# First block's feed-forward in plain float32, and the split of its weights moved eight units later

## The chip, the cores and the metric

One core of a Trainium2 chip runs the whole program. The metric is the device time of one execution in microseconds (us). Three runs of the kernel before took 1052.34, 1054.83 and 1055.13 us, median 1054.83. Readings come from one more execution with the hardware profiler on: 1054.6 us, of which the profile spans 1052.9.

## The reference

Three stages follow each other. A delta rule over 768 steps for 4 x 8 heads of width 48, then two feed-forward networks on 3072 tokens (model width 384, hidden width 2048):

```python
for t in range(S):
    y[:, :, t] = einsum('bhd,bhde->bhe', q[:, :, t], state)
    v_old = einsum('bhde,bhd->bhe', state, k_n[:, :, t])
    state = state + beta_t * einsum('bhd,bhe->bhde', k_n[:, :, t], v_t - v_old)
# x: the y of all heads, (3072, 384)
h = x @ w_in;  g = h if h >= 1, 0 if h <= -1, else (h + 1)**2 / 4;  x2 = g @ w_out
h = x2 @ w2_in; r = max(h, 0); out = (r * r) @ w2_out
```

All is float32, except that the weights reach the kernel as int64 bit patterns of float64 values, two 32-bit words for each weight.

## The kernel before

**The delta rule** goes in 24 chunks of 32 steps. A chunk needs the inverse of a 32x32 triangular matrix for every batch and head. `tri` makes these for a group of chunks at once: DVE (the VectorE) normalises the gram matrix, and then some 30 dependent steps multiply and add ever other shapes of it, each step one multiply (L411) and one add (L412). Group 0 (two chunks) is done on DVE in two half-size inverses side by side and put together with two small matmuls (`joined`: z at L437, w at L445). All other groups go through the steps on GpSimd (POOL). With the inverse, `chunk_steps` runs a chunk as six pieces: ks and tr (the new values u), qs and pu (the output y), ku (the state in PSUM, tiles `sps`), xt (y transposed to x). The pieces of a chunk follow each other through PE, ACT and DVE.

**The feed-forward** goes in blocks of 2 or 3 chunks (256 or 384 tokens). A block has 16 units, one for each 128 hidden columns: `hidden` (h, three K tiles of 128) and, two units later (LAG), `out1` (three output tiles in PSUM, `acc`). A float32 product is made of three float32r products: x and w are each split in a rounded part and a remainder (`xh`, `xl`; the two halves of `weight`; `gh`, `gl`), and `prods` issues hi*hi, lo*hi, hi*lo: 9 matmuls for h, 9 for acc. The chunks of the next block run between the units of this one, so the first block (chunks 0 and 1) has to wait for nothing but its own two chunks, and the units of block 0 and 1 also carry the work that follows.

**The weights.** 32 tiles (16 units x 2 matrices) of the first network are loaded as raw words (`load_w`, L157, 384 KB each), turned into float32 by one ACT instruction (L164) and two DVE instructions (L172, L175), and split by one ACT copy (L186) and one DVE subtraction (L190). Eighteen loads are asked for at the start (EAGER), the others as conversions go on (AHEAD). The second network's weights are converted later and wait in DRAM (w2f).

**What sets the order.** Up to the first `manual_schedule` block's end every engine follows the written order. After it PE alone follows the written order, and a scheduler orders the other engines' queues by its own model of their times. Each engine runs its queue in order, so an instruction that waits holds all behind it. SP issues the DMAs, also in order. Work that is hung on unit slots (`put`, two slots for each unit; `later` puts it behind that unit's own instructions) sets when the next chunks, the inverses and the weights come.

Of the kernel before, what the change touches and what calls it, by code (L numbers as in the profile page):

```python
# [25 lines left out]
def kernel(  # L26
# [38 lines left out]
    EAGER = 18  # L65
    AHEAD = 8
# [48 lines left out]
    kqt, kvt, gp, nt, xh, xl = {}, {}, {}, {}, {}, {}  # L115

# [31 lines left out]
    raws = {}  # L148


    def load_w(x, key):
# [5 lines left out]
        nc.sync.dma_start(raw.rearrange("p a b -> p (a b)"), (w1, w2)[w][f, i].bitcast(I32))  # L157


    def convert_stages(key, box):  # L160
        def s0():
# [6 lines left out]
        def s1():  # L168
# [13 lines left out]
    def part_stages(key, box):  # L182
        _, f, i = key

        def s3():
            nc.scalar.copy(weight(i, f)[0], box["t"])  # L186

        def s4():
            hi, lo = weight(i, f)
            nc.vector.tensor_sub(lo, box["t"], hi.bitcast(F32))  # L190

        return convert_stages(key, box) + [s3, s4]
# [3 lines left out]
    def weight_items(w):  # L196
# [5 lines left out]
        def item(x):  # L202
            _, f, i = keys[x]
            box = {}
            if w == 0:
                r = part_stages(keys[x], box)
            else:
                r = convert_stages(keys[x], box)
                r.append(lambda: nc.sync.dma_start(w2f[f, :, i], box["t"]))
            s1 = r[1]  # L210
            r[1] = lambda: (s1(), ahead(x + 1 + (RAW if w else AHEAD)))
# [5 lines left out]
        def ahead(end):  # L217
            while todo and todo[0][0] < end:
# [49 lines left out]
    def gram(c, lo=0, hi=2, late=0, eng=None):  # L268
# [18 lines left out]
        if c >= KQ:  # L287
            kqg.pop(c)
            if late < 2:
# [23 lines left out]
    spare = {  # L313
        name: f"w{i}{NF - f}" for name, i, f in
        (("u0", 1, 1), ("u1", 1, 2), ("cross", 0, 1), ("z", 1, 3), ("l", 0, 2), ("d", 1, 4))
    }
# [17 lines left out]
    def tri(n, eng, halves=False):  # L334
# [9 lines left out]
        def two(t, rows, cols):  # L344

            a = t[:, rows, cols]
            (ps_, p_), (rs_, r_), (cs_, c_) = a.ap
            return bass.AP(a.tensor, a.offset, [[ps_, p_], [T2 * (T + 1), 2], [rs_, r_], [cs_, c_]])

# [5 lines left out]
        both = slice(0, T2)  # L355
# [16 lines left out]

        def row():
            if halves:
                d = two(gm, both, both)
                eng.tensor_mul(
                    d, d, r.rearrange("p (a o i) -> p a o i", a=2, o=1)
                    .to_broadcast([P, 2, T2, T2]))
                return
            for e, rs, cs in whole:  # L380
                e.tensor_mul(gm[:, rs, cs], gm[:, rs, cs], across(r, rs, cs))

        def row2():
            if halves:
                eng.tensor_mul(
                    two(x, both, both), two(gm, both, both),
                    g.rearrange("p (a i o) -> p a i o", a=2, o=1).to_broadcast([P, 2, T2, T2]))
            else:
                for e, rs, cs in whole:
                    e.tensor_mul(x[:, rs, cs], gm[:, rs, cs], down(g, rs, cs))  # L390
# [5 lines left out]
        def step(j):  # L396
            if halves:
                w = T2 - 1 - j
                t = ring.tile([P, 2, j, w], F32, tag="t0", bufs=1, name="t")
                rest = two(x, slice(0, j), slice(j + 1, T2))  # L400
                by = two(x, slice(0, j), slice(j, j + 1))
                of = two(gm, slice(j, j + 1), slice(j + 1, T2))
                shape = [P, 2, j, w]
            else:
                w = T - 1 - j
                t = ring.tile([P, j, w], F32, tag="t0", bufs=1, name="t")
                rest = x[:, 0:j, j + 1:T]
                by = x[:, 0:j, j:j + 1]
                of = gm[:, j:j + 1, j + 1:T]
                shape = [P, j, w]  # L410
            eng.tensor_mul(t, by.to_broadcast(shape), of.to_broadcast(shape))  # L411
            eng.tensor_add(rest, rest, t)  # L412
# [44 lines left out]
    def chunk_steps(c):  # L457
# [75 lines left out]
        def xt():  # L533
            if j == 0:
                xh[n] = ring.tile([P, KT, P * SIZES[n]], F32R, tag="xh", bufs=2, name="xh")
# [6 lines left out]
            nc.scalar.copy(xh[n][:, :, cols], o)  # L542
            marks[2] = nc.vector.tensor_sub(xl[n][:, :, cols], o, xh[n].bitcast(F32)[:, :, cols])  # L543
# [19 lines left out]
    marks = [None, None, None]  # L563

    def hidden(layer, n, f):
# [4 lines left out]
        wi = weight(0, f)  # L570
        cols = [slice(kt * P, (kt + 1) * P) for kt in range(KT)]
        prods([
            (h, (wi[0][:, c], wi[1][:, c]), (xh[n][:, kt], xl[n][:, kt]), kt == 0, kt == KT - 1)
            for kt, c in enumerate(cols)
        ])
        r = ring.tile([P, w], F32, tag="rg", bufs=RG, name="r")
        g = ring.tile([P, w], F32, tag="rg", bufs=RG, name="g")
        if layer == 0:
# [10 lines left out]
        def rest():  # L589
            ghi = ring.tile([P, w], F32R, tag="gh", bufs=GB, name="gh")  # L590
# [12 lines left out]
    def out1(n, f):  # L603
        w = P * SIZES[n]
        if f == 0:
            acc[n] = [ps.tile([P, w], F32, tag=f"acc{m}", name=f"acc{m}") for m in range(KT)]
        g = gs.pop((0, n, f))
        wo = weight(1, f)
        cols = [slice(m * P, (m + 1) * P) for m in range(KT)]
        prods([  # L610
            (acc[n][m], (wo[0][:, c], wo[1][:, c]), g, f == 0, f == NF - 1)
            for m, c in enumerate(cols)
# [294 lines left out]
```

## Time and profile before

| | |
|---|---|
| median of three runs | 1054.83 us |
| profiled execution: time, span | 1054.6 us, 1052.9 us |
| PE busy (matmul) | 989.3 us, 94% |
| DVE busy | 611.5 us, 58% |
| ACT busy | 454.3 us, 43% |
| POOL busy | 313.2 us, 30% |
| first h matmul of block 0 | at 65.68 us |
| first h matmul of block 1 | at 137.93 us |
| first h matmul of block 2 | at 199.90 us |

Times in the profile are microseconds from the start of the span. PE works through two records for one small float32 matmul and one record for one float32r matmul. "issue" behind a row is time in which the engine waited for nothing that the profile shows.

### The profile page before, as it was taken

The page shows a single profiled execution, that of the slowest core. Times are in us where ns is not written, and L with a number is a line of the kernel's source. Part 1 is how long each engine was busy: PE and PEld are TensorE (multiplying, and loading weights), DVE is VectorE, ACT ScalarE, POOL GpSimd, SP SyncE. Part 2 cuts the span into 40 slices and gives each one's busy share as a digit, 9 for nine tenths or more (in the row PEclk, how much of TensorE's full clock was granted, in tenths as well). Part 3 has the DMA queues.
Part 4 walks back from the last instruction along what each step waited for, and adds up shares of the span by engine and source line. Part 5 has one row for each costly group of instructions (what it writes and reads, how often), then busy time and mean ns, then how long its engine had stood idle before and what let it go on. Part 6 is the DMA issues. An engine that isn't in the chain of part 4 may idle for free.

```text
span 1052.9 us, 33012 instructions
## 1 busy us (share of the span) xinstructions
PE 989.3 (94%) x14440; PEld 945.0 (90%) x14440; DVE 611.5 (58%) x1125; ACT 454.3 (43%) x931; POOL 313.2 (30%) x456
## 2 busy tenths in 40 slices
PE   4358898999999999999999999999999999999998
PEld 4347788898899998999999999999999999999998
DVE  6879765675575666767545577543434343444333
ACT  2346544445444444545445554433333333333332
POOL 4690681294039208608600123110101010010000
PEclk9997999999999999999999999999999999999999
DMA  9942144352451441512111223010101010000000
GB/s 297 326 121 77 33 124 134 88 150 73 130 152 48 148 134 33 167 56 70 31 42 55 77 90 121 16 45 1 45 1 46 1 45 1 24 1 24 1 23 23
DMA packets 36049, 80.89 MB, mean 77 GB/s; under 512 B 4544, under 2 KB 18368, under 8 KB 35904
## 3 DMA queue, kind: packets, MB, share of 16 engines
q1 hardware_dynamic: 35904, 78.78, 24.8%
q8 instruction: 113, 1.85, 0.8%
q14 instruction: 32, 0.26, 0.1%
HBM read 63.03 MB, written 15.73 MB: 75 GB/s over the span
## 4 chain that ended last, share of the span: by engine, by line
PE 81%; DVE 11%; issue 4%; ACT 2%; DMA 1%; SPq 0%; DVEq 0%; ACTq 0%
PE acc L555 36%; PE h L555 35%; PE tr L486 2%; PE yy L506 2%; PE sps L517 2%; PE yy L472 2%; DVE g L582 1%; DVE g L584 1%; PE g L281 1%; PE ks L472 1%; DVE gl L593 1%; DVE wl L172 1%; DVE wl L175 1%; DVE gp L415 1%; PE xt L540 1%
## 5 line engine op out<-in xcount | busy, mean ns | idle before, releaser
L555 PE MATMUL h<-xh,w 128*128 128x384 f32 (+1 forms) x1632 | 320.4, 332 | 1.8 <-ACT r L581 1.3
L555 PEld LDWEIGHTS h<-xh,w 128*128 128x128 f32 x1632 | 272.7, 190 | 6.8 <-ACT r L581 1.8
L593 DVE TENSOR_TENSOR gl<-g,gh 128x384 fp32r<-128x384 f32 (+1 forms) x272 | 169.5, 623 | 134.3 <-ACT gh L592 128.8
L592 ACT CAST gh<-g 128x384 fp32r<-128x384 f32 (+1 forms) x272 | 135.0, 496 | 209.3 <-DVE g L584 106.0
L555 PE MATMUL h<-xl,w 128*128 128x384 f32 (+1 forms) x816 | 179.8, 329 | 1.3 <-DVE xl L543 1.3
L555 PE MATMUL acc<-gh,w 128*128 128x384 f32 (+1 forms) x864 | 168.5, 331 | 3.8 <-ACT gh L592 3.8
L587 DVE TENSOR_TENSOR g<-r 128x384 f32<-128x384 f32 x128 | 71.4, 558 | 157.4 <-ACT r L586 157.4
L555 PE MATMUL acc<-w,gh 128*128 128x384 f32 x768 | 155.6, 337 | 2.0 <-DVE e L600 2.0
L586 ACT ACTIVATE r<-h,zero 128x384 f32<-128x384 f32 x128 | 74.5, 582 | 166.1 <-PE h L555 166.1
L555 PEld LDWEIGHTS acc<-gh,w 128*128 128x128 f32 x864 | 136.9, 191 | 9.8 <-ACT gh L592 4.2
L555 PEld LDWEIGHTS h<-xl,w 128*128 128x128 f32 x816 | 141.5, 190 | 1.9 <-DVE xl L543 1.9
L555 PEld LDWEIGHTS acc<-w,gh 128*128 128x128 f32 x768 | 136.3, 188 | 2.3 <-ACT gh L592 2.3
L581 ACT ACTIVATE r<-h,one 128x384 f32<-128x384 f32 (+1 forms) x144 | 78.6, 546 | 89.4 <-PE h L555 84.9
L411 POOL TENSOR_TENSOR t<-tx,gm 128x30 f32<-128x30 f32 (+9 forms) x180 | 109.6, 609 | 19.9 <-DVE tx L390 6.4
L412 POOL TENSOR_TENSOR tx<-tx,t 128x30 f32<-128x30 f32 (+9 forms) x180 | 108.4, 602 | 13.7
L584 DVE SCALAR_TENSOR_TENSOR g<-r,g 128x384 f32<-128x384 f32 (+1 forms) x144 | 88.8, 617 | 36.6 <-ACT g L583 34.8
L582 DVE TENSOR_SCALAR g<-r 128x384 f32<-128x384 f32 (+1 forms) x144 | 63.6, 442 | 79.5 <-ACT r L581 78.9
L642 POOL CAST xh<-x2r 128x1152 fp32r<-128x1152 f32 x8 | 9.5, 1186 | 292.9 <-PE h L555 246.1
L583 ACT ACTIVATE g<-g 128x384 f32<-128x384 f32 (+1 forms) x144 | 70.6, 490 | 59.4 <-DVE g L582 58.3
L555 PE MATMUL acc<-gl,w 128*128 128x384 f32 (+1 forms) x432 | 91.5, 320 | 2.6 <-DVE gl L593 2.6
L555 PE MATMUL acc<-w,gl 128*128 128x384 f32 x384 | 88.0, 337 | 0.0
L555 PEld LDWEIGHTS acc<-gl,w 128*128 128x128 f32 x432 | 72.4, 190 | 3.3 <-DVE gl L593 3.3
(94 smaller groups left out, 835.9 us busy)
## 6 DMA issues: line engine op xcount, KB each, us to landing
raw<-in_w_dram SPq DMA_DIRECT2D x64, 384.0 KB, 6.3
kqt<-in_kq_dram SPq DMA_DIRECT2D x88, 192.0 KB, 3.8
kv<-in_kv_dram SPq DMA_DIRECT2D x24, 384.0 KB, 3.1
w2f<-wl SPq DMA_DIRECT2D x32, 192.0 KB, 3.5
w2r<-w2f SPq DMA_DIRECT2D x16, 384.0 KB, 3.0
x2r<-x SPq DMA_DIRECT2D x8, 576.0 KB, 4.4
out_dram<-e SPq DMA_DIRECT2D x24, 192.0 KB, 2.0
x<-e SPq DMA_DIRECT2D x18, 192.0 KB, 2.3
```

The costliest lines, as they stand in the source:

```text
L411: eng.tensor_mul(t, by.to_broadcast(shape), of.to_broadcast(shape))
L412: eng.tensor_add(rest, rest, t)
L472: per_bh(lambda b, h, p, pd: nc.tensor.matmul(o[p, h], kqt[c][pd, b // 2, h, x * T:(x + 1) * T], st[pd, b // 2, h], start=h == 0, stop=x = ...
L555: nc.tensor.matmul(o, *((r, l) if swap else (l, r)), **flags)
L581: marks[0] = nc.scalar.activation(r, h, AF.Relu, bias=one)
L582: marks[1] = nc.vector.tensor_scalar(g, r, 2.0, 0.5, ALU.min, ALU.mult)
L583: nc.scalar.activation(g, g, AF.Square)
L584: nc.vector.scalar_tensor_tensor(g, r, -1.0, g, ALU.add, ALU.max)
L586: marks[0] = nc.scalar.activation(r, h, AF.Relu, bias=zero)
L587: marks[1] = nc.vector.tensor_mul(g, r, r)
L592: nc.scalar.copy(ghi, g)
L593: nc.vector.tensor_sub(glo, g, ghi.bitcast(F32))
```

## The change

In block 0 `hidden` and `out1` issue plain float32 matmuls, three for h and three for acc, on the converted weights (w32), on x as ACT copies it out of PSUM (one float32 tile, no xl) and on g (one float32 tile, no gl). Its activation has one ACT instruction more and one DVE instruction fewer. A converted weight stays in its place, and `parts` copies it eight units later by a DMA into a buffer of the ring `wt` (3 buffers), from where ACT and DVE make the two parts that block 1 needs.

Around it: 12 loads at the start instead of 18; load 12 goes into the tile that `cross` holds, and all later loads are queued behind it. Group 0's inverse is cut in two halves, one on DVE and one on POOL. The masks of the gram matrices move from POOL to DVE. The written order now reaches to the end of chunk 1 on all engines.

```diff
-    EAGER = 18
-    AHEAD = 8
+    EAGER = 12
+    OWN = 17
+    SPLIT = 8
...
     def load_w(x, key):
...
-        if w == 0:
+        if w == 0 and x < OWN:
             pool, tag, bufs = wp, f"w{i}{f}", 1
...
+        if w == 0 and x == EAGER:
+            after[0] = lambda: tc.issue_after(ins.ins)
...
+            dst = bits
+            if w == 0:
+                w32[i, f] = wp.tile([P, 2, DM], F32, tag=f"w{i}{f}", name=f"w{i}{f}")[:, 1]
+                dst = w32[i, f].bitcast(I32)
             nc.vector.scalar_tensor_tensor(
-                bits, t, 3, bits, ALU.logical_shift_left, ALU.bitwise_or
+                dst, t, 3, bits, ALU.logical_shift_left, ALU.bitwise_or
             )
...
+    def parts(i, f):
+        box = {}
+        def s0():
+            box["t"] = tmp("wt", WT)
+            nc.sync.dma_start(box["t"], w32.pop((i, f)))
+        def s1():
+            nc.scalar.copy(weight(i, f)[0], box["t"])
+        def s2():
+            hi, lo = weight(i, f)
+            nc.vector.tensor_sub(lo, box["t"], hi.bitcast(F32))
...
         def ahead(end):
+            if w == 0 and turn[0] is not None:
+                end = min(end, EAGER)
...
+        if halves:
+            parts = [(e, *[slice(T2 * i, T2 * i + T2)] * 2) for i, e in enumerate(halves)]
...
+    def plain(o, w, x, **flags):
+        nc.tensor.matmul(o, w, x, **flags)
...
+        if first:
+            for kt, c in enumerate(cols):
+                plain(h, w32[0, f][:, c], xh[n][:, kt], start=kt == 0, stop=kt == KT - 1)
...
+                nc.scalar.activation(g, r, AF.Relu, scale=-0.5, bias=one)
+                nc.scalar.activation(g, g, AF.Square, scale=-1.0, bias=one)
...
+            for m, c in enumerate(cols):
+                plain(acc[n][m], w32[1, f][:, c], g, start=f == 0, stop=f == NF - 1)
...
-        begin, pre, steps, end = tri(0, V, True)
+        begin, pre, steps, end = tri(0, V, (V, G))
...
-        masks = [gram(c, 1, 2, late=2, eng=G) for c in range(HEADS)]
+        masks = [gram(c, 1, 2, late=2) for c in range(HEADS)]
...
+        end()
+        more_w1(1)
+        for c in range(HEADS):
+            ld0(c)
+        go(masks1)
+        more_w1(3)
...
+        first1(EAGER + RAW)
+        quiet(load_kv, HEADS)
...
+        for f in range(NF):
+            for i in range(2):
+                load, *split = parts(i, f)
+                put(0, 2 * (f + SPLIT) + i - 1, load)
+                put(0, 2 * (f + SPLIT) + i, *later(*split))
```

Three places of the queues show what moves. First SP's queue near the start, where `raw` are the weight loads; before:

```order
L132 DMA kqt<-in_kq_dram 48x1024 x8
L141 DMA kv<-in_kv_dram 128x768 x2
L157 DMA raw<-in_w_dram 128x768 x19
L141 DMA kv<-in_kv_dram 128x768
L132 DMA kqt<-in_kq_dram 48x1024 x2
L157 DMA raw<-in_w_dram 128x768 x2
L132 DMA kqt<-in_kq_dram 48x1024 x2
L157 DMA raw<-in_w_dram 128x768 x8
```

And after, around the thirteenth weight load, each with its waits (DMAHW: an earlier DMA):

```order
L162 DMA raw<-in_w_dram 128x768 [waits DMAHW1_49]
L162 DMA raw<-in_w_dram 128x768 [waits DMAHW2_49]
L162 DMA raw<-in_w_dram 128x768 [waits DMAHW3_49,PE_49,Activation_49]
L162 DMA raw<-in_w_dram 128x768 [waits DMAHW4_49]
L162 DMA raw<-in_w_dram 128x768 [waits DMAHW5_49]
L143 DMA kv<-in_kv_dram 128x768 [waits DMAHW6_49]
L134 DMA kqt<-in_kq_dram 48x1024 [waits DMAHW7_49]
```

Nineteen weight loads stood in one piece without a wait for an engine. Now the thirteenth waits for PE, the last reader of `cross`, and everything that follows in SP's queue stands behind it.

Second DVE's queue just ahead of the first g of block 0 (L584 before, L609 after). Names such as w16 are matrix 1, unit 6. Before:

```order
L190 TENSOR_TENSOR w06_1140<-wl_1132,w06_1140 128x384
L175 SCALAR_TENSOR_TENSOR wl_1182<-wt_1177,wl_1182 128x384
L190 TENSOR_TENSOR w15_1170<-wl_1142,w15_1170 128x384
L172 TENSOR_SCALAR wl_1284<-raw_136 128x384
L190 TENSOR_TENSOR w07_1180<-wl_1172,w07_1180 128x384
L172 TENSOR_SCALAR wl_1306<-raw_138 128x384
L175 SCALAR_TENSOR_TENSOR wl_1284<-wt_1187,wl_1284 128x384
L584 SCALAR_TENSOR_TENSOR g_1120<-r_1119,g_1120 128x256
```

After:

```order
L192 SCALAR_TENSOR_TENSOR w15_1237<-wt_1150,wl_1235 128x384
L185 TENSOR_SCALAR wl_1304<-raw_1096 128x384
L192 SCALAR_TENSOR_TENSOR w07_1251<-wt_1241,wl_1249 128x384
L185 TENSOR_SCALAR wl_1352<-raw_1239 128x384
L192 SCALAR_TENSOR_TENSOR w16_1306<-wt_1255,wl_1304 128x384
L185 TENSOR_SCALAR wl_1374<-raw_1253 128x384
L192 SCALAR_TENSOR_TENSOR w08_1354<-wt_1310,wl_1352 128x384
L609 SCALAR_TENSOR_TENSOR gh_1115<-r_1110,g_1111 128x256
```

The subtractions (L190) are gone from this place. Sixteen whole conversions stand ahead of the first g.

Third DVE's queue where group 1's inverse is handed on (gp<-tx) and chunk 2's values (kv<-kv,ks) are made. Before:

```order
L415 STREAM_TRANSPOSE gp_253<-tx_79 128x32x32
L190 TENSOR_TENSOR w014_1744<-wl_1729,w014_1744 128x384
L172 TENSOR_SCALAR wl_1775<-raw_1550 128x384
L172 TENSOR_SCALAR wl_1826<-raw_1569 128x384
L190 TENSOR_TENSOR w113_1773<-wl_1746,w113_1773 128x384
L593 TENSOR_TENSOR gl_1723<-g_1717,gh_1722 128x256
L482 TENSOR_TENSOR kv_1101<-kv_1101,ks_1789 128x384
```

After, where L211 is the subtraction of `parts`:

```order
L421 STREAM_TRANSPOSE gp_243<-tx_79 128x32x32
L211 TENSOR_TENSOR w10_1590<-wt_1576,w10_1590 128x384
L185 TENSOR_SCALAR wl_1619<-raw_1559 128x384
L211 TENSOR_TENSOR w01_1615<-wt_1592,w01_1615 128x384
L185 TENSOR_SCALAR wl_1669<-raw_1582 128x384
L488 TENSOR_TENSOR kv_1098<-kv_1098,ks_1630 128x384
```

The splits of unit 0 and 1 now stand where those of unit 13 and 14 stood.

## Rows read from the trace of the kernel before

**Rows 1.** Busy time by stretch: PE, PEld, DVE, ACT, POOL, granted clock, DMA share, GB/s
```profile
30.00:40.00 10.00, 2.52 (x158) 2.33 (x159) 8.88 (x20) 3.00 (x8) 4.24 (x7) 1.00 1.05 312
80.00:90.00 10.00, 8.65 (x162) 7.82 (x161) 10.00 (x27) 8.36 (x20) 1.18 (x3) 0.65 0.23 79
200.00:1053.00 853.00, 843.65 (x10406) 812.24 (x10404) 464.56 (x824) 364.56 (x723) 214.43 (x296) 1.00 0.19 59
```
**Rows 2.** Timeline of PE, opening: start, us, engine, line, operation [idle before <-releaser]
```profile
33.07 1.52 PE L437 MATMUL z<-d,l 32*32 32x16 f32 x98 [2.31 <-issue]
...
41.19 1.52 PE L445 MATMUL w<-gp,z 32*32 32x16 f32 x98 [6.21 <-issue]
...
48.36 1.00 PE L486 MATMUL tr<-kv,gp 32*32 32x48 f32 x34 [5.03 <-issue]
...
56.13 0.92 PE L506 MATMUL yy<-u,gp 32*32 32x48 f32 x34 [4.07 <-issue]
...
79.03 1.65 PE L555 MATMUL acc<-gh,w 128*128 128x256 f32 x6 [3.28 <-ACT gh L592]
```
**Rows 3.** The page's engine totals, and its instruction queue: packets, MB, share
```profile
PE 989.3 (94%) x14440; PEld 945.0 (90%) x14440; DVE 611.5 (58%) x1125; ACT 454.3 (43%) x931; POOL 313.2 (30%) x456
...
q8 instruction: 113, 1.85, 0.8%
```
**Rows 4.** Timeline of DVE, opening and first g
```profile
27.02 2.07 DVE L415 STREAM_TRANSPOSE gp<-tx 128x1024 f32<-128x1024 f32 x1
28.98 1.01 DVE L433 STREAM_TRANSPOSE d<-tx 128x512 f32<-128x512 f32 x1
29.84 1.95 DVE L351 STREAM_TRANSPOSE gm<-gp 128x1024 f32<-128x1024 f32 x1
...
34.01 0.68 DVE L381 TENSOR_TENSOR gm<-gm,st 128x512 f32<-128x512 f32 x1
...
41.89 0.29 DVE L450 TENSOR_TENSOR gp<-gp,w 128x128 f32<-128x128 f32 x1 [2.42 <-PE w L445]
...
77.49 1.04 DVE L584 SCALAR_TENSOR_TENSOR g<-r,g 128x256 f32<-128x256 f32 x1
```
**Rows 5.** Conversions on DVE from 66 to 80 us: count, busy us, mean ns
```profile
L175 DVE SCALAR_TENSOR_TENSOR wl<-wt,wl 128x384 int32<-128x384 int32 x6 | 4.7, 798 | 0.0
L172 DVE TENSOR_SCALAR wl<-raw 128x384 int32<-128x384 uint32 x7 | 4.6, 662 | 0.0
```
**Rows 6.** The same from 82 to 102 us
```profile
L175 DVE SCALAR_TENSOR_TENSOR wl<-wt,wl 128x384 int32<-128x384 int32 x11 | 6.1, 552 | 0.0
L172 DVE TENSOR_SCALAR wl<-raw 128x384 int32<-128x384 uint32 x10 | 3.5, 354 | 0.0
```
**Rows 7.** Timeline of POOL, first and last step of group 1's inverse
```profile
37.41 0.48 POOL L411 TENSOR_TENSOR t<-tx,gm 128x30 f32<-128x30 f32 x1 [1.43 <-DVE tx L390]
...
80.29 0.66 POOL L412 TENSOR_TENSOR tx<-tx,t 128x30 f32<-128x30 f32 x1
```
**Rows 8.** Timeline of PE at full clock, and the waiting tr of chunk 2
```profile
101.53 1.10 PE L281 MATMUL g<-kqt 48*32 48x64 f32 x64
...
104.78 0.87 PE L555 MATMUL h<-xh,w 128*128 128x256 f32 x6
...
105.84 0.87 PE L555 MATMUL acc<-gh,w 128*128 128x256 f32 x6
...
109.29 0.88 PE L472 MATMUL ks<-st,kqt 48*32 48x48 f32 x64
...
114.65 1.50 PE L486 MATMUL tr<-kv,gp 32*32 32x48 f32 x64 [3.21 <-DVE kv L482]
...
137.93 0.84 PE L555 MATMUL h<-xh,w 128*128 128x256 f32 x6
```
**Rows 9.** DMA issues: weight loads up to 70 us, w2f over the span: count, size, us to landing
```profile
raw<-in_w_dram SPq DMA_DIRECT2D x33, 384.0 KB, 8.2
...
w2f<-wl SPq DMA_DIRECT2D x32, 192.0 KB, 3.5
```

More of the change, by code (lines that the diff above doesn't have):

```diff
@@ L288, in gram @@
             kqg.pop(c)
-            if late < 2:
+            if turn[0] is None:
                 load_kg(c + KG)
@@ L311 @@
     cross = {}
[L313 to L316, printed above, removed]
+    spare = {"cross": f"w1{EAGER // 2 - 1}"}
+    for x, name in enumerate(("u0", "u1", "z", "l", "d", "t")):
+        spare[name] = f"w{x % 2}{NF - 1 - x // 2}"
     def cross_gram(a, c):
@@ L371, in gamma2 @@
             return nc.vector.tensor_mul(g, g, bet[:, n, :])
+        parts = whole
+        if halves:
+            parts = [(e, *[slice(T2 * i, T2 * i + T2)] * 2) for i, e in enumerate(halves)]
         def row():
[L374 to L380, printed above, removed]
+            for e, rs, cs in parts:
                 e.tensor_mul(gm[:, rs, cs], gm[:, rs, cs], across(r, rs, cs))
         def row2():
[L384 to L390, printed above, removed]
+            for e, rs, cs in parts:
+                e.tensor_mul(x[:, rs, cs], gm[:, rs, cs], down(g, rs, cs))
             nc.vector.tensor_copy(flat(x), g)
@@ L396, in step @@
         def step(j):
[L397 to L412, printed above, removed]
+            ts = []
+            for i, e in enumerate(halves or (eng,)):
+                lo, hi = (T2 * i, T2 * i + T2) if halves else (0, T)
+                w = hi - lo - 1 - j
+                pool, tag = (wp, spare["t"]) if i else (ring, "t0")
+                t = pool.tile([P, j, w], F32, tag=tag, bufs=1, name="t")
+                ts.append((e, lo, hi, t))
+                e.tensor_mul(
+                    t,
+                    x[:, lo:lo + j, lo + j:lo + j + 1].to_broadcast([P, j, w]),
+                    gm[:, lo + j:lo + j + 1, lo + j + 1:hi].to_broadcast([P, j, w]),
+                )
+            for e, lo, hi, t in ts:
+                rest = x[:, lo:lo + j, lo + j + 1:hi]
+                e.tensor_add(rest, rest, t)
         def end():
@@ L589, in rest @@
         def rest():
+            if first:
+                return
             ghi = ring.tile([P, w], F32R, tag="gh", bufs=GB, name="gh")
@@ L607, in out1 @@
         g = gs.pop((0, n, f))
-        wo = weight(1, f)
+        wo = weight(1, f) if n else None
         cols = [slice(m * P, (m + 1) * P) for m in range(KT)]
-        prods([
-            (acc[n][m], (wo[0][:, c], wo[1][:, c]), g, f == 0, f == NF - 1)
-            for m, c in enumerate(cols)
-        ])
+        if n:
+            prods([
+                (acc[n][m], (wo[0][:, c], wo[1][:, c]), g, f == 0, f == NF - 1)
+                for m, c in enumerate(cols)
+            ])
+        else:
+            for m, c in enumerate(cols):
+                plain(acc[n][m], w32[1, f][:, c], g, start=f == 0, stop=f == NF - 1)
         if f == NF - 1:
@@ L663, in go, with quiet @@
         return r
+    def quiet(load, c):
+        with after[0]():
+            load(c)
     V, G = nc.vector, nc.gpsimd
@@ L712 @@
             save0(c)
-        go([gram(c, late=2, eng=G) for c in range(GFIRST[1], GFIRST[2])])
+        masks1 = [gram(c, late=2) for c in range(GFIRST[1], GFIRST[2])]
         cross_gram(0, 1)
-        masks = [gram(c, 1, 2, late=2, eng=G) for c in range(HEADS)]
+        masks = [gram(c, 1, 2, late=2) for c in range(HEADS)]
         go(steps)
```

105 lines of the change are left out of this document (58 added, 47 removed).

## The prediction

> **What bounds the kernel now.** I read the busy time by stretch first [rows 1]. After 200 us PE is busy 843.65 of 853 us: there only PE's own work counts, and the change leaves that work alone. So whatever block 2 starts earlier or later is the change of the whole time. I then read PE's timeline from the left [rows 2] and asked what each part waits for.
>
> Up to the first h, PE waits for nothing that the profile shows four times: 2.31, 6.21, 5.03 and 4.07 us [rows 2], 17.6 us in a chain in which z, w, tr and yy follow each other. The pauses come at even distances. PE's 14440 matmuls (with as many weight loads) go with 113 packets of instructions, 1.85 MB [rows 3]: one packet of 16 KB for every 128 matmuls. The pauses lie about 128 matmuls apart, in a stretch where the DMA engines are full (share 1.05 [rows 1]) and a weight load takes 8.2 us to land [rows 9]. I read them as PE waiting for its next instructions behind weight loads.
>
> From there to about 114 us DVE sets the pace: 10.00 of 10 us from 80 to 90 [rows 1]. The first g is finished by DVE only at 78.5 [rows 4], and acc starts at 79.03 [rows 2], although its h was there long before. While POOL runs group 1's inverse, until 80.95 [rows 7], one conversion on DVE (two instructions) costs 0.662 + 0.798 = 1.46 us [rows 5]; without POOL 0.354 + 0.552 = 0.91 [rows 6]. Neighbours overlap by some 0.1 us, as the starts and lengths in [rows 4] show (27.02 + 2.07 against 28.98), so I count 1.3 and 0.75 us.
>
> **Part 1, the opening.** The end of group 0's inverse stays at 27 us [rows 4]: DVE has half the elements in each step but POOL now runs the other half in 28 small instructions, and its small one takes 0.48 us [rows 7], 13 us in all. Bounds: at DVE's 0.29 [rows 4] 5 us less, at POOL's 0.66 [rows 7] 5 us more. I take no change.
>
> From 27 us DVE has, in its written order: d and gp, 1.01 + 2.07; four masks of 128x512, for which I take 0.68 each from the like operation in [rows 4], 2.7; three conversions without POOL, 2.7 at most; two small subtractions, 0.6; then group 1 from its transpose to the scaled matrix, as before from 29.84 to 34.69 [rows 4], 4.85; within it two masks, chunk 1's subtraction and the second scaling, 2.4 (0.6 each, by the 0.68). Sum 16.3, so DVE reaches the fourth conversion at 43.3. For this PE must deliver w and ks in time. With 12 loads instead of 18 and the thirteenth waiting for `cross`, about 8 MB are asked for until then, 26 us at 312 GB/s [rows 1]: the traffic ends at about 27. Then PE's pauses shrink; without the first two (8.5 us) w's subtraction comes at 33.4 instead of 41.89 [rows 4], earlier than DVE's turn at 35. Bound above: the pauses all stay (rival 2).
>
> From 43.3 on, 13 conversions stand ahead of the first g. POOL starts group 1's steps there too, so they cost 1.3 each: 16.9, and g 0.6. acc starts at 61.5 with the passing of semaphores, against 79.03: 17.5 us earlier. The loads don't bind: conversion 13 comes at about 55, and its load is asked for at about 43 and lands within 8.2 [rows 9].
>
> **Part 2, from acc of unit 0 to acc of unit 4.** DVE has ten more conversions (13.0), two masks, one copy of the state and four g (5.0 together at POOL's price): 18 us, to 79.5. PE has four units and three small groups there; its clock was 0.65 in the like stretch of before [rows 1], for which I add 1: 80.5.
>
> **Part 3, the plain matmul.** The trace has no 128x128 float32 product, only small ones of two records each. At full clock 64 records of 64 columns take 1.10 us and 64 of 48 columns 0.88 [rows 8]. If four tiles run side by side, the difference is 0.22/16 = 13.7 ns for 16 columns, 0.86 ns a column, with 14 ns fixed: 234 ns for 256 columns, and six records (three matmuls) take 1.40 us. If only two run side by side it is half, 0.7 us. Nine float32r matmuls take 105.84 - 104.78 = 1.06 us [rows 8], 118 ns each. Bounds for a group: 0.7 (one record as quick as one float32r) to 1.75 (a quarter above the value). I take 1.40, since the tiles of tr and yy occupy four separate quarters: 0.34 us more for each of 32 groups, 10.9 us of added PE work, of which part 1 and 2 hide what stands under DVE.
>
> The row gives two records for one matmul and no more. The Trainium skill ("FP8 and Floating Point Precision", TensorE Precision Notes) says true FP32 takes four passes through the array. That would make four of 118 ns for one matmul, an estimate of 1.42 us for a group: it speaks against the change, which trades three passes for four, and the trace agrees if four tiles run side by side.
>
> **Part 4, from acc of unit 4 to block 1.** PE is the bound: 19 groups (10 acc, 9 h) at 1.40 + one gram 1.1 + ten small groups of chunks 2 and 3 at 0.88, less overlaps, 9.7 together = 36.3. Its tr waits for chunk 2's subtraction, 3.21 us before [rows 8]. After, group 1's steps on POOL end at 43.3 + 43.5 [rows 7] = 87, and g of unit 9, the transpose, two splits and two half conversions stand ahead of the subtraction: about 96, when PE is there at 93. I keep 3.5 us of waits, and 1.5 for DVE, which has 12 splits and 6 conversions more than the units' own work there. Block 1 starts at 121.8, against 137.93 [rows 8]: 16 us earlier.
>
> **Part 5, block 1.** The 32 splits (one DMA, one ACT and one DVE instruction each, the last 0.6 us, between [rows 5] and [rows 6]) are as many as before but now lie in units 8 to 24. About 18 of them fall in block 1, 11 us of DVE beside its own work, with group 2's steps on POOL in part of it. I take 3 us lost; bounds 0 and 9. Block 2 starts 13 us earlier than before. What the first block no longer does (16 subtractions for g, one DVE instruction a unit, two for x) lies inside parts 1 and 2.
>
> **Sum.** Block 1 16.1 us earlier (17.5 from part 1, of which parts 2 to 4 give back 1.4), part 5 gives back 3: 13.1. From the profiled execution's 1054.6 that is 1041.5; that execution lies 0.2 below the median, so the forecast is 1042.
>
> **Rivals.**
> 1. *More is gained* (chance 0.16): the record of float32 is as quick as float32r's, or the port between POOL and DVE costs less. Then part 4 shrinks by 19 x 0.7 = 13, of which POOL's end at 87 and the chain to tr give back about 5: 1034. With conversions at 1.0 instead of 1.3 the first acc comes 4 us earlier; both together 1030. For: the times of 32- and 48-row tiles are equal (0.88), which fits another limit than the columns. Against: the growth from 48 to 64 columns.
> 2. *The pauses stay* (0.10). If PE's pauses are not its instructions, ks still ends at about 51.4 (48.36 + 1 + copy + 1.5), DVE starts the 13 conversions at 54 and the first acc comes at 72: 7 earlier, of which parts 2 to 5 give back 4.4: 1052, no change. The 16 KB per 128 matmuls speak against it.
>    The Trainium skill ("Runtime: NRT & Kernel Launch", Instruction fetch mechanics) says that crossing a 16 KiB block of instructions is mostly hidden; by that rule the pauses have another cause, and it is this rival's 1052. The trace disagrees in this stretch, with pauses of up to 6.21 us.
> 3. *The splits' ring* (0.10, slower). The splits and the last six conversions share the three buffers of `wt`. A split holds one from its DMA's issue to its subtraction: landing + 1.5 us. With 3.5 to land (the like 192 KB transfer [rows 9]) this is 5, and 38 holders go through three buffers in 38 x 5/3 = 63 us from 88 on, in time for the last user at about 188. With 8.2 [rows 9] it is 9.7 and they end at 211: PE waits 23 us, 13 gained, 1064. It decides from 7.9 us a hold. Against it: in that stretch the DMA queues are far from full, and the weight loads thin out.
> 4. *Block 1 takes it back* (0.12): DVE is full until POOL ends group 2 near 140, and units 12 to 24 run at DVE's pace, 9 us lost instead of 3 and 2 more in part 4: 1050.
>
> The forecast has the rest, 0.52, with a range of its own from 1035 to 1048.
>
> **Numbers.** What a measurement of this kernel can tell from no change is about 0.3%, 3 us. Faster by more: the forecast, rival 1 and three quarters of rival 4, 0.77. Within: most of rival 2, the rest of rival 4 and a little of rival 3, 0.12. Slower: 0.11. The range 1027 to 1054 leaves out rival 3 and the far end of rival 1.
>
> **What would show it.** Right: no idle "issue" over 2 us on PE between z and the first h; first h near 48 and first acc near 61.5 with DVE without a gap before it; nine-matmul groups of 1.06 replaced by groups of about 1.40 at full clock; block 1 at 122, block 2 at 187, and from there the same PE time as before. Wrong: pauses of 4 us and more that remain (rival 2); groups of 0.7 (rival 1); ACT's or DVE's part of a split waiting on the copy's DMA while PE waits for block 1's weights (rival 3); g or gl late behind splits in block 1 (rival 4).

## The result, and the profile after

Four runs of the changed kernel took 1062.59 to 1070.83 us, median 1068.41; four of the kernel before, on the same chip, 1052.34 to 1056.02, median 1054.98. The ratio is 1.0129 with a 95% interval of 1.0101 to 1.0157: slower, by 13.4 us, where 13 us faster was forecast. The profiled execution is the longest of the four, 1070.83 us with a span of 1069.1.

First the page's totals of the changed kernel and its instruction queue, against [rows 3]:

```profile
PE 1002.7 (94%) x14344; PEld 948.4 (89%) x14344; DVE 606.3 (57%) x1097; ACT 456.3 (43%) x931; POOL 311.9 (29%) x480
...
q8 instruction: 112, 1.84, 0.7%
```

The totals hardly differ from before, and tell nothing of 13 us. The timeline of PE in the opening does; it answers to [rows 2]:

```profile
31.06 1.51 PE L443 MATMUL z<-d,l 32*32 32x16 f32 x98 [1.53 <-issue]
...
34.94 1.51 PE L451 MATMUL w<-gp,z 32*32 32x16 f32 x97 [1.98 <-issue]
...
38.82 1.00 PE L492 MATMUL tr<-kv,gp 32*32 32x48 f32 x35 [1.74 <-issue]
...
46.74 0.61 PE L472 MATMUL yy<-u,cross 32*32 32x48 f32 x36 [1.64 <-issue]
...
51.14 6.05 PE L574 MATMUL h<-xh,w 128*128 128x256 f32 x18 [0.57 <-ACT xh L550]
...
65.49 2.93 PE L574 MATMUL acc<-gh,w 128*128 128x256 f32 x6
...
83.41 2.93 PE L574 MATMUL h<-xh,w 128*128 128x256 f32 x6 [6.39 <-ACT r L598]
...
96.42 1.46 PE L574 MATMUL h<-xh,w 128*128 128x256 f32 x6
97.72 1.46 PE L574 MATMUL acc<-gh,w 128*128 128x256 f32 x6
...
139.96 0.57 PE L548 MATMUL xt<-ident,kv 128*128 128x128 f32 x3 [4.27 <-ACT kv L516]
...
142.53 1.62 PE L564 MATMUL h<-xh,w 128*128 128x256 f32 x6
...
216.01 1.20 PE L564 MATMUL h<-xh,w 128*128 128x384 f32 x6
```

The opening gained as meant: the four pauses are 6.9 us together instead of 17.6 (a fifth of before, 1.43 us at 60.34, makes it 19.1), the first h comes 14.5 us earlier and the first acc 13.5 us earlier. Then the lead melts. There is a hole of 6.39 us at 83 us; block 1 starts at 142.53 instead of 137.93; block 2, at 216.01 instead of 199.90, is 16.1 us late. From there both kernels need 853 us. So the loss lies between 65 and 216 us. Busy time of the changed kernel by stretch (columns as in [rows 1]):

```profile
80.00:90.00 10.00, 6.59 (x76) 5.15 (x77) 5.58 (x9) 3.97 (x8) 7.06 (x15) 0.66 0.86 272
142.53:216.01 73.48, 62.45 (x1510) 57.06 (x1508) 42.51 (x93) 34.26 (x81) 7.78 (x15) 0.90 0.49 149
200.00:1053.00 853.00, 847.45 (x10742) 815.28 (x10741) 468.85 (x832) 367.06 (x732) 215.49 (x296) 1.00 0.20 60
```

And of the kernel before, for its block 1:

```profile
137.93:199.90 61.97, 57.25 (x1515) 52.85 (x1514) 36.89 (x76) 27.75 (x67) 21.15 (x34) 0.97 0.46 130
```

The two rows at the block's own times hold the same work of PE, 1510 and 1515 matmul records, but the changed kernel takes 73.48 us for it instead of 61.97, although DVE (42.5 of 73.5 us) and ACT (34.3) are far from full. No engine is the bound there: something waits. Of the 11.5 us, PE is idle for 6.3 (11.0 instead of 4.7) and busy for 5.2 more (62.45 instead of 57.25), since its granted clock is 0.90 instead of 0.97. The timeline has the same six matmuls at about half speed behind a wait of PE, and at full speed some us later:

```profile
162.32 0.90 PE L548 MATMUL xt<-ident,kv 128*128 128x128 f32 x3 [3.50 <-ACT kv L516]
162.88 1.63 PE L564 MATMUL h<-xh,w 128*128 128x256 f32 x6
...
168.19 0.87 PE L564 MATMUL h<-xh,w 128*128 128x256 f32 x6
```

The granted clock is 0.50 (1.2 GHz) from 162.88 to 165.00 and 1.00 (2.4 GHz) from 168 to 170. From 80 to 90 DVE, full before [rows 1], is busy 5.58 of 10. The waits of ACT in the changed kernel from 40 to 220 us (what waited, for what: us in total, times, the longest):

```profile
ACT w L207 <- DMA wt<-w: 25.1, 17, 3.0
...
ACT wt L177 <- DMA raw<-in_w_dram: 9.1, 7, 2.9
```

ACT's queue at the end of block 0 shows whom the first of these hurts:

```profile
134.66 0.51 ACT L207 CAST w<-wt 128x384 fp32r<-128x384 f32 x1 [3.02 <-DMA wt<-w]
...
138.64 0.51 ACT L207 CAST w<-wt 128x384 fp32r<-128x384 f32 x1 [2.51 <-DMA wt<-w]
139.05 0.47 ACT L529 COPY st<-sps 128x384 f32<-128x384 f32 x1
139.42 0.48 ACT L516 COPY kv<-yy 128x384 f32<-128x384 f32 x1
```

L207 is the first half of a split (`parts`, s1). The one at 134.66 is the 13th of 32, for unit 6 of block 1; with 16 units in 73.5 us from 142.53 on, PE needs it near 170 us, so its own lateness costs nothing. But it stands at the head of ACT's queue until the DMA copy has landed, and behind it stands L516, which hands y to the transposes (xt) at 139.96: PE's 4.27 us. The chain of waits of the changed kernel says the same (start, us, what):

```profile
134.21 4.41 DMA wt<-w
138.61 0.02 issue
138.64 0.51 ACT w L207
139.15 0.38 ACT st L529
139.53 0.39 ACT kv L516
139.92 0.04 issue
139.96 0.33 PE xt L548
```

In block 1 the same chain has three more landings, 12.4 us together, each with L207 and the rest of ACT's queue behind it:

```profile
156.59 4.76 DMA wt<-w
...
175.13 5.12 DMA wt<-w
...
182.71 2.57 DMA wt<-w
```

Why the copy comes so late is in the waits of SP from 100 to 200 us, and how long the splits go on in the tile view of `wt`:

```profile
SPq L204 <- DVE w L211: 41.0, 15, 10.9
```

```profile
L204 SPq DMA_DIRECT2D wt<-w x32: 464/471/1190, 78.3 to 182.7; - x32
L207 ACT CAST w<-wt x32: 494/512/522, 98.3 to 185.3; 128x384 fp32r<-128x384 f32 x32
L211 DVE TENSOR_TENSOR w<-wt,w x32: 546/559/1047, 100.8 to 186.4; 128x384 fp32r<-128x384 f32 x32
```

A copy starts only when the subtraction (L211) of an earlier split has given back one of the three buffers; with a landing of 3.3 us (median) it is often not there when ACT asks for it.

### The profile page after: what moved, and what is told of

The parts are those of the page before. It is cut to its first block, busy times and chain, and to the rows that moved or that the text cites. A ratio compares the mean times of both kernels' runs of the same rounds, so it can differ in the third digit from the quotient of the medians.

```text
span 1069.1 us, 32882 instructions
## 1 busy us (share of the span) xinstructions
PE 1002.7 (94%) x14344; PEld 948.4 (89%) x14344; DVE 606.3 (57%) x1097; ACT 456.3 (43%) x931; POOL 311.9 (29%) x480
## 4 chain that ended last, share of the span: by engine, by line
PE 82%; DVE 7%; DMA 4%; issue 3%; ACT 2%; SPq 1%; DVEq 0%; ACTq 0%
PE acc L564 35%; PE h L564 34%; PE g L302 2%; DMA wt<-w 2%; PE tr L492 2%; PE yy L478 2%; PE acc L574 1%; PE yy L512 1%; DMA raw<-in_w_dram 1%; PE sps L523 1%; PE ks L478 1%; PE h L574 1%; DVE wl L185 1%; DVE g L600 1%; DVE g L609 1%
## 5 line engine op out<-in xcount | busy, mean ns | idle before, releaser
L564 PE MATMUL h<-xh,w 128*128 128x384 f32 (+1 forms) x1536 | 305.6, 335 | 3.1 <-ACT r L598 3.1
L564 PEld LDWEIGHTS h<-xh,w 128*128 128x128 f32 x1536 | 260.3, 190 | 7.0 <-ACT r L598 3.5
L622 DVE TENSOR_TENSOR gl<-g,gh 128x384 fp32r<-128x384 f32 (+1 forms) x256 | 160.6, 627 | 132.1 <-ACT gh L621 129.0
L564 PE MATMUL h<-xl,w 128*128 128x384 f32 (+1 forms) x768 | 170.7, 331 | 1.3 <-DVE xl L552 1.3
L564 PE MATMUL acc<-gh,w 128*128 128x384 f32 (+1 forms) x768 | 152.5, 334 | 0.0
L564 PEld LDWEIGHTS acc<-gh,w 128*128 128x128 f32 x768 | 124.0, 190 | 4.9 <-DVE e L629 0.3
L411 POOL TENSOR_TENSOR t<-tx,gm 128x84 f32<-128x84 f32 (+18 forms) x194 | 111.2, 573 | 19.6 <-DVE tx L397 5.3
L418 POOL TENSOR_TENSOR tx<-tx,t 128x84 f32<-128x84 f32 (+18 forms) x194 | 111.3, 574 | 15.0
L609 DVE SCALAR_TENSOR_TENSOR g<-r,g 128x384 f32<-128x384 f32 (+1 forms) x128 | 82.5, 645 | 33.5 <-ACT g L601 31.8
L564 PE MATMUL acc<-gl,w 128*128 128x384 f32 (+1 forms) x384 | 82.3, 323 | 0.0
L278 POOL TENSOR_TENSOR kv<-kv,nt 128x384 f32<-128x384 f32 x24 | 21.9, 914 | 191.8 <-DMA kv<-in_kv_dram 157.7
```

Of the source, the lines that this page charges most:

```text
L411: e.tensor_mul(t, x[:, lo:lo + j, lo + j:lo + j + 1].to_broadcast([P, j, w]), gm[:, lo + j:lo + j + 1, lo + j + 1:hi].to_broadcast([P, j, w]),
L418: e.tensor_add(rest, rest, t)
L564: nc.tensor.matmul(o, *((r, l) if swap else (l, r)), **flags)
L609: ins = nc.vector.scalar_tensor_tensor(last, r, -1.0, g, ALU.add, ALU.max)
L622: nc.vector.tensor_sub(glo, g, ghi.bitcast(F32))
```

## The experiments

Three theories. **A:** ACT's in-order queue stands at the copy's transfer and holds what PE waits for. **B:** the added work (plain products; fuller ACT and DVE) costs it. **C:** the weight loads come late (load 12 waits for `cross`, loads from 17 on go through the ring of three). All ratios are against runs of the kernel before on the same chip in the same job. The table has times of the profiled execution (first acc, first x transposes of block 1, first h of block 2) beside the median of all runs. These are single executions, up to 6 us from the median (e11), and each edit lets the scheduler order the queues of ACT, DVE and POOL anew; 2 or 3 us between neighbours need not be the edit's own. The intervals of e2, e3, e5, e7 and e15 overlap that of the changed kernel, so their times alone hardly tell them from it.

| | first acc | xt, block 1 | h, block 2 | median | ratio, interval |
|---|---|---|---|---|---|
| before | 79.03 | 136.58 | 199.90 | | |
| changed | 65.49 | 139.96 | 216.01 | 1068.41 | 1.0129, 1.0101 to 1.0157 |
| e1_act | 65.44 | 137.01 | 200.72 | 1055.82 | 1.0018, 1.0003 to 1.0034 |
| e2_pool | 64.53 | 131.33 | 210.48 | 1066.30 | 1.0120, 1.0096 to 1.0145 |
| e3_own25 | 63.54 | 134.49 | 208.35 | 1063.47 | 1.0093, 1.0069 to 1.0118 |
| e5_eager16 | 67.66 | 138.62 | 210.15 | 1066.67 | 1.0127, 1.0087 to 1.0168 |
| e4_act_own | 63.43 | 134.87 | 199.27 | 1057.10 | 1.0030, 1.0014 to 1.0046 |
| e6_mix | 62.67 | 127.13 | 192.84 | 1050.46 | 0.9958, 0.9939 to 0.9976 |
| e6_again | 62.33 | 128.18 | 195.53 | 1051.89 | 0.9979, 0.9960 to 0.9998 |
| e7_slot | 63.02 | 138.60 | 208.41 | 1065.29 | 1.0100, 1.0083 to 1.0118 |
| e8_before12 | 81.10 | 139.53 | 199.61 | 1055.25 | 1.0007, 0.9994 to 1.0021 |
| e10_mix_ring | 64.82 | 131.94 | 200.71 | 1053.85 | 1.0003, 0.9986 to 1.0019 |
| e11_gate | 76.51 | 133.75 | 193.96 | 1053.68 | 0.9988, 0.9975 to 1.0002 |
| e12_mix10 | 63.09 | 130.14 | 197.18 | 1054.88 | 1.0004, 0.9992 to 1.0017 |
| e15_cast_pool | 65.54 | 132.74 | 205.36 | 1062.55 | 1.0088, 1.0057 to 1.0118 |

**e1_act: the copy by ACT instead of a transfer.**

```diff
-            nc.sync.dma_start(box["t"], w32.pop((i, f)))
+            nc.scalar.copy(box["t"], w32.pop((i, f)))
```

> The copy of a converted weight into the ring is made by ACT instead of a DMA (32 ACT instructions of 0.5 us more, 32 DMAs fewer); the rest as in the changed kernel. Theory A, the loss sits in ACT's queue, where the split's first instruction waits for the copy's DMA (25.1 us in 17 waits from 40 to 210 us) and holds r, kv and xh behind it: those waits go, block 2 starts 12 to 20 us earlier than at 216, about 1050 us. Theory B, the loss is the added work (PE's 7.7 us for 32 groups of 1.30 instead of 1.06, and DVE and ACT fuller in units 8 to 24): ACT gets 16 us more of it, so no gain, 1065 to 1075. Theory C, the loss comes from weight loads that land late in units 1 to 4: no change, 1063 to 1070.

Measured 1055.82: by the medians 12.6 us less than the changed kernel (by the two ratios 1.1%, 11.7 us) through this one line, though ACT has 32 instructions more. In block 1 (from its transposes to block 2's h) it takes 63.7 us, the kernel before 63.3, the changed kernel 76.1. PE's granted clock in block 1 is 1.00 again. Block 2 is 15.3 us earlier, as A says (12 to 20); the time is not A's 1050, because the opening's lead is gone by block 1 all the same. The line takes out the whole transfer: ACT's wait for it, SP's wait for the ring and the DMA traffic. That ACT's queue is the path is read from the chain above, and tested once more in e15.

**e2_pool: the copy by POOL.**

```diff
-            nc.sync.dma_start(box["t"], w32.pop((i, f)))
+            nc.gpsimd.tensor_copy(box["t"], w32.pop((i, f)))
```

> The same copy made by POOL, whose queue is busy with the steps of an inverse for most of units 8 to 20. Theory A says that what hurts is any wait for a remote producer in ACT's queue: the waits on the DMA turn into waits on POOL, part of the loss stays, 1055 to 1065, more than with the copy on ACT. Theory B: ACT's and PE's load are unchanged and DVE gets more port conflicts, 1068 to 1075. Theory C: no change, 1063 to 1070.

Measured 1066.30, above A's range, for another reason. Block 1's transposes come 5.2 us before those of the kernel before. Then PE stands still near 172 us (first PE, then DVE, of this run):

```profile
184.58 1.50 PE L492 MATMUL tr<-kv,gp 32*32 32x48 f32 x64 [12.73 <-issue]
```

```profile
182.50 1.98 DVE L421 STREAM_TRANSPOSE gp<-tx 128x1024 f32<-128x1024 f32 x1 [6.35 <-POOL tx L418]
```

POOL runs group 2's inverse, one dependent step after the other, with the copies in the same queue: from 80 to 190 us they are busy for 18.6 us, with 14.7 us of waits before them, and the inverse is handed on at 182.5. tr needs it: here, too, what stands in the queue holds what is behind it, on another engine.

**e3_own25: weights 17 to 24 loaded into their own tiles. e5_eager16: 16 loads at the start.**

```diff
-    OWN = 17
+    OWN = 25
```

```diff
-    EAGER = 12
+    EAGER = 16
```

> Weight loads 17 to 24 go into tiles of their own instead of a ring of three, so they need not wait for a conversion; the DMA copies stay. Theory C, late loads cost the 6.4 us wait for r at 77 to 83 us and the slow units 1 to 4: acc of unit 4 comes 6 to 8 us earlier than at 91.3 and the time falls to 1058 to 1062. Theory A: the loads of units 1 to 4 are a small part, and what they give is lost again at the splits, 1063 to 1070. Theory B: no change.

> Sixteen weight loads are asked for at the start instead of twelve, before the wait for cross; cross goes into another tile. My reading of the opening, PE's pauses between z and the first h are instruction packets that wait behind weight loads: four more loads, 1.6 MB, last some 4 to 5 us longer, PE's pauses after 27 us grow by 3 to 6 us in all and the first h comes that much later than 51.1. If the pauses have another cause they stay at 1.5, 2.0, 1.7 and 1.6 us. Theory C gains 4 us at the loads of units 1 and 2; the time 1062 to 1070 by A and B, 1060 to 1064 by C.

e3 takes 4.9 us off by the medians (1063.47), 3.8 by the ratios, at the edge of what can be told. ACT's waits for weight loads up to 84 us fall from 9.1 to 3.1 us, and the hole before the h at 83 us from 6.39 to 3.88; acc of unit 4 comes 3.9 us earlier (87.42), where C gave 6 to 8. ACT still waits 24.0 us for the copies. So C seems a part, and a smaller one than A. e5 gives nothing that can be told from the changed kernel (1066.67); its pause before z grows from 1.53 to 4.00 us, its four pauses from 6.9 to 8.9 and its first h comes at 51.89, less than expected for 4 more loads in the opening.

**e4_act_own: e1 and e3 together.**

> Two edits together: ScalarE makes the copy (as in the run that gave 1055.8), and the loads of weights 17 to 24 go to tiles of their own. Theory A (the copy's transfer in ScalarE's queue) has been paid already and says nothing of the second edit. Theory C (late weight loads): alone, the second edit took 4.9 us off 1068.4; with the copy on ScalarE it takes about as much again, 1051 (1048 to 1053), with block 1's first x transposes at about 133 instead of 137.0. Theory B (the two engines that convert are simply fuller between 105 and 137 us): whatever arrives earlier waits for VectorE and ScalarE there, so little is left, 1054 to 1057, with the transposes still at 136 to 137.

Measured 1057.10: nothing beyond e1. Block 1 comes 2.1 us earlier than in e1, and block 2 still 1.5 us, but a wait of 1.6 us between 420 and 500 us, which e1 does not have, takes it back. The time is the one that B gave, the transposes (134.87) lie between B's and C's: the earlier loads bring 2.0 us at the first acc and not more than that later, where C expected about 5.

**e6_mix, and e6_again: POOL copies for 16 weights, ACT for the others, with the own tiles (OWN = 25); e10_mix_ring: the same without them; e12_mix10: POOL for 20 weights.**

```diff
-            nc.sync.dma_start(box["t"], w32.pop((i, f)))
+            (nc.gpsimd.tensor_copy if f < 8 else nc.scalar.copy)(box["t"], w32.pop((i, f)))
```

> As the run with ScalarE's copy and weights 17 to 24 in own tiles, but the copies of weights 0 to 15 (units 8 to 15, until about 135 us) are made by GpSimd and only the later ones by ScalarE. Theory B: ScalarE and VectorE are relieved where they are full, so block 1's transposes come near 131 us, where they came with GpSimd's copies throughout, and the triangular solve on GpSimd still ends before PE needs it (172 us), since half of the copies are gone: 1047 (1044 to 1050). Against it: if the solve on GpSimd is late all the same, a hole of PE of up to 12.7 us comes back near 170 us, and the time is 1055 to 1062.

> GpSimd copies weights 0 to 15, ScalarE 16 to 31, weights 17 to 24 loaded through the ring of three as in the changed kernel. With the loads in own tiles the same mix took 1050.5. Theory B (engines between 105 and 160 us decide, not the loads): 1050 to 1052, block 1's transposes at 128 to 131 us. Theory C (late loads count once the engines are relieved): 1053 to 1056, transposes at 131 to 133.

> As the mix that took 1050.5, with GpSimd copying weights 0 to 19 instead of 0 to 15. Between 127 and 148 us the mix lost 5 us against the kernel before, with ScalarE's copies and VectorE's subtractions in the chain: if ScalarE's share of that counts, 1047 to 1050; if GpSimd's solve, which ended at 166 us and is needed at 172, is now late, 1052 to 1058 with a hole of PE near 170 us.

> The mix that took 1050.5 once more, for its interval: 1049 to 1052 and all of the interval below 1 if it is a better version than both, about 1054 if the first look was luck (the run with 20 weights on GpSimd, one step away, gave 1054.9, the one without the own tiles 1053.9).

e6 took 1050.46, and 1051.89 the second time. Block 1 starts some 9 us before that of the kernel before, and the inverse is in time (DVE's transpose of it at 166.3). PE's two longest waits from 106 to 140 us in e6:

```profile
PE tr L492 <- DVE kv L488: 3.2, 2, 2.0
PE xt L548 <- ACT kv L516: 0.9, 1, 0.9
```

In the changed kernel tr waits 4.1 there and xt 6.2. So with both queues free of long waits a little is gained: the two ratios lie below 1 with their whole intervals, by 0.2 and 0.4%, at the edge of what can be told. e10 and e12, one step away on either side, are no different from the kernel before. By the medians e10 is 2 to 3 us slower than the two runs with own tiles, as C expected, but its interval overlaps that of e6_again. e12 has no hole of PE, and its block 1 starts 3 us later than e6's.

**e7_slot: ACT's and DVE's part half a unit later in their queues, the transfer as it was.**

```diff
-                put(0, 2 * (f + SPLIT) + i, *later(*split))
+                put(0, 2 * (f + SPLIT) + i + 1, *later(*split))
```

> The changed kernel with the copy still a transfer, but ScalarE's and VectorE's parts of the split put one half-unit (about 2 us) later in their queues. Theory A (what costs is that the queue stands at a transfer that has not landed): ScalarE's waits for the copy fall from 25 us to under 8, and the time to 1057 to 1061. If instead the transfers themselves cost (DMA traffic) or the added work does, the waits fall and the time stays at 1066 to 1069. If the three buffers of the copies bind instead, the wait only moves to the next transfer's start: 1064 to 1069 with a wait for a free buffer in place of the one for the landing.

Measured 1065.29, the third outcome in time: ACT waits as long as before, in fewer and longer waits (40 to 220 us), for what is later in the queue also gives back its buffer later.

```profile
ACT w L207 <- DMA wt<-w: 25.6, 14, 4.1
```

The wait stayed the one for the landing, though, and not one for a free buffer as the expectation had it: the buffer is waited for by SP.

**e15_cast_pool: ring and transfer as in the changed kernel, but POOL makes the rounded part of 16 weights.**

```diff
-            nc.scalar.copy(weight(i, f)[0], box["t"])
+            cast = nc.gpsimd.tensor_copy if f < 8 else nc.scalar.copy
+            cast(weight(i, f)[0], box["t"])
```

> The changed kernel with the copy still a transfer into the ring of three, but for weights 0 to 15 GpSimd instead of ScalarE makes the rounded part from it; so GpSimd's queue stands at the transfers in units 8 to 15, ScalarE's does not. If the loss is the wait at the head of ScalarE's queue: PE's waits for ScalarE between 106 and 140 us fall from 6.2 to under 2 us, block 1's first x transposes come at 131 to 134 us instead of 139.96, though a buffer is held as long as before. The end depends on GpSimd's solve, which is held by the same waits: 1060 to 1064 if it is done by 172 us, up to 1072 with a hole of PE near 175 us if not. If the ring's three buffers are the loss (rival 3 of the prediction as it was priced), the transposes stay at 139 to 140.

Measured 1062.55, transposes at 132.74: both as A expects. POOL now stands at the transfers (its waits from 80 to 190 us):

```profile
POOL w L208 <- DMA wt<-w: 8.4, 5, 2.6
```

From 106 to 140 us ACT has no such wait, and PE's waits there are these two:

```profile
PE h L575 <- ACT r L599: 1.7, 1, 1.7
PE tr L493 <- DVE kv L489: 1.5, 1, 1.5
```

With the same ring and the same transfers, block 1 starts 7.2 us earlier. So it is what stands in ACT's queue, and not the ring as such. Not all of the 7.2 us need be the wait: 16 casts of 0.5 us have left ACT as well, and no run took only these away; e1, where ACT has more to do and no such wait, starts block 1 2.9 us earlier. Afterwards, with the casts of units 16 to 23 on ACT, ACT waits 8.6 us for the copies again, and block 1 takes 72.6 us against 63.3 before.

**e8_before12 and e11_gate: the opening alone, on the kernel before.** e8 changes only the number of loads at the start; e11 also makes the thirteenth wait for `cross`, and the others stand behind it.

```diff
-    EAGER = 18
+    EAGER = 12
...
+        if w == 0 and x == EAGER:
+            after[0] = lambda: tc.issue_after(ins.ins)
...
+            if w == 0 and turn[0] is not None:
+                end = min(end, EAGER)
...
+    spare["cross"] = f"w1{EAGER // 2 - 1}"
```

> The kernel before with 12 instead of 18 weight loads issued in the opening, and nothing else. If the pauses of PE's opening come from the weights queued in front of the instruction packets, they shrink here too (from 19 us in five pauses towards 7 in the changed kernel) with no plain float32 anywhere; the first h comes at 55 to 60 us instead of 65.7, and the time is 1044 to 1050 if the rest keeps the gain, or 1053 to 1056 if the conversions set the first acc in any case (then first acc stays near 79 us). If the pauses had another cause (the program's length), they stay and the time is 1054.

> The kernel before with the changed kernel's opening alone: 12 weight loads, and the 13th in the tile that the opening still uses, so that it and those behind it can't start before the opening is done (the run with 12 loads and no such tile left the DMA as full as before). No plain float32. If the weights on the DMA make the pauses: DMA share in 0 to 50 us falls from 1.0 to 0.6, the pauses from 20 us to 7, first h at 52 to 54 us. The conversions (five instructions a weight here, and the 13th weight late by some 10 us) then hold block 0: first acc at 75 to 80 us and time 1053 to 1060. If the pauses come from the length of the program, they stay above 15 us.

In e8 the DMA share from 0 to 50 us stays at 1.00: the later loads had no reason to wait and went out early all the same, and so the pauses stayed (20.5 us for all five, and a first acc at 81.10). It tested nothing but that. In e11 the traffic does go down:

```profile
0.00:50.00 50.00, 23.20 (x1024) 20.68 (x1024) 40.11 (x81) 15.89 (x35) 25.50 (x51) 1.00 0.70 202
```

and so do the pauses:

```profile
34.54 1.51 PE L446 MATMUL z<-d,l 32*32 32x16 f32 x98 [3.69 <-issue]
...
38.27 1.52 PE L454 MATMUL w<-gp,z 32*32 32x16 f32 x98 [1.82 <-issue]
...
62.28 1.65 PE L564 MATMUL h<-xh,w 128*128 128x256 f32 x6 [0.61 <-ACT xh L551]
...
76.51 1.65 PE L564 MATMUL acc<-gh,w 128*128 128x256 f32 x6 [3.11 <-ACT gh L601]
```

to 6.0 us (a third has 0.46), with no plain float32 in the kernel. But the first h comes at 62.28, not at 52 to 54: tr there waits 5.94 us for DVE. The first acc is 2.5 us earlier than before and the time no different (1053.68; the profiled execution, 1047.97, is the shortest of ten). So of the 13.5 us that the changed kernel gains to the first acc, only 2.5 come with fewer loads alone; the others need the shorter work of DVE as well, or the new written order, which was not tried apart.

## Why the prediction was wrong, step by step

Block 2 was to start at 186.8 us (199.90 - 13.1) and started at 216.01, 29.2 us late: parts 1, 2, 4 and 5 missed by 4.0, 6.8, 9.9 and 8.5. In e1, without the transfer, block 2 starts at 200.72. So by these two executions 13.9 of the 29.2 us are there without the transfer, and they alone leave no gain; the other 15.3, 3.5 of them before block 1 and 11.8 in it, make the kernel slower than before. Three steps failed: "the loads don't bind", with DVE as the bound (parts 1 and 2); the waits of PE, sized too small (part 4); and the 3 us for the splits, in which a wait for the copy's landing cost nothing (part 5).

**Part 1 held, but for 4 us.** The pauses went as forecast (none of 2 us or more), the first h came at 51.14 for "near 48", and the first acc 13.5 us earlier for 17.5. Two things were late: DVE's first conversions wait for ACT (2.64 us at 33.35 and 0.52 at 34.70 on DVE's timeline; the fourth starts at 45.13 and not at 43.3), and the step "the loads don't bind" was wrong. The thirteenth load went out at 47.44, when PE had last read `cross`, and not at about 43; on the chain of waits to the first acc a load that was asked for at 52.52 takes 8.76 us to land. These are the loads behind load 12, in ACT's queue of the changed kernel:

```profile
61.36 0.55 ACT L177 ACTIVATE wt<-raw 128x384 f32<-128x384 f32 x1 [2.94 <-DMA raw<-in_w_dram]
...
76.55 0.55 ACT L177 ACTIVATE wt<-raw 128x384 f32<-128x384 f32 x1 [1.46 <-DMA raw<-in_w_dram]
...
79.21 0.56 ACT L177 ACTIVATE wt<-raw 128x384 f32<-128x384 f32 x1 [1.35 <-DMA raw<-in_w_dram]
```

I checked the landing of one load and not the rate of twenty: from 50 to 80 us the DMA share is 0.93 to 0.96, as full as the opening was before.

**Part 2 missed 6.8 us more.** Acc of unit 4 came at 91.31 for 80.5; before it lies the hole of 6.39 us behind late loads. I had DVE as the bound there; DVE waited.

**Part 3 held.** A plain group takes 1.30 us at full clock (90.02 to 91.31, 96.42 to 97.72 on PE's timeline), within the bounds and nearer the value (1.40) than the low end (0.7): 0.24 us more than three float32r products, 7.7 for 32 groups. The row contradicts rival 1, and so do the conversions, its other half: 0.65 + 0.91 us each from 50 to 82 us, not less than before. One plain matmul then is 433 ns, 3.7 times the 118 ns of a float32r one; the Trainium skill's four passes ("FP8 and Floating Point Precision", TensorE Precision Notes) gave an estimate of 1.42 for the group, a little above the measurement.

**Part 4 missed 9.9 us more.** From acc of unit 4 to block 1's first h it took 51.2 us, not 41.3. In e1, without the transfer's waits, it still took 48.3 (90.73 to 139.03), so 2.9 of the miss is A's and 7.0 was there anyway. Of the 7.0, waits of PE for ACT and DVE (9.0 from 106 to 140 in e1, where I had allowed 5) explain 4; the other 3 I can't put down to one thing. That e6 took 43.6 there (85.63 to 129.26) points to relief of ACT as worth most of it, as B has it; e6 differs in its loads, too.

**Part 5 missed 8.5 us, and its mechanism was wrong.** "I take 3 us lost; bounds 0 and 9": block 1, from first h to first h, took 73.5 us instead of 62.0, so 11.5 were lost, beyond the bound; in e1 it took 61.7. I counted the splits as work of DVE and ACT that fits in their free time. The time that counts is not the 0.5 us of the ACT instruction but the up to 3 us that it stands at the head of the queue, and PE's lower clock behind the waits, 5.2 of the 11.5 us. That the waits bring the clock down is not shown apart; in e1 both are gone together. Even without this part's miss the kernel would have been no faster: block 1 started 4.6 us later than before (142.53 for 137.93).

**Rival 3 had the place and the wrong price.** It named the copy, its landing, the ring of three and the wait on the copy's DMA, at 1064 and a chance of 0.10, and made it harmless below 7.9 us a hold. A hold was below that: the copy on the chain at 115.17 takes 4.90 us and its subtraction ends at 121.69, 6.5 us. The splits did end in time, at 187 for the 188 of the prediction; PE waits for no weight between 40 and 220 us. What I left out is who else stands in the queue of the instruction that waits. The sign that the prediction gave for this rival was a split that waits on the copy while PE waits for block 1's weights; PE waited for r and kv, which stand behind the split on ACT, and which it needs at once.

Rival 4 (block 1 gives it back) had the place, too, but neither the cause nor the sign: DVE is busy 42.5 of 73.5 us there, and PE waits for no g or gl. Rival 2 is refuted by the opening, and by e11.

## What to carry to other kernels

Where work is put on an in-order engine with a wait for a transfer, price the wait by everything behind it in that queue, not by its own deadline: a wait that is harmless for its own result cost some 12 us here, and they came back when the waiting engine copied the same 192 KB itself. A ring that the consumer's end frees makes the producer start late each time, so moving the consumer back in its queue does not give the transfer more time (e7). And an early lead is only worth what the next bound passes on: 13.6 to 16.4 us at the first acc were 0 at block 1 in e1, 5 in e10 (copies shared by ACT and POOL) and 9 in e6 (loads relieved as well).

## What the runs showed of the hardware that was not expected

- A copy of 192 KB within SBUF by DMA takes 3.3 us (median) from issue to landing, and up to 5.1 on the chain, with the DMA engines about half busy (0.52 from 100 to 200 us); the same copy takes ACT 0.51 us (e1) and POOL 0.63 (e2), both medians of 32.
- The pauses of PE in the opening depend on the DMA traffic and not on the number of instruction packets: with 113 packets and a DMA share of 0.99 from 0 to 50 us they are 19.1 us (all five), in the changed kernel with 112 and 0.58 they are 6.9, and in e11, with 113 and 0.70, 6.0.
